# Start of a fused linear-attention and GEGLU kernel: weights' ends loaded once, loads reordered, one tile's statistics moved to ScalarE

## The chip, the cores and the metric

The kernel runs on one core of a Trainium2 chip. A core has a matrix engine (TensorE, PE in the profile), a vector engine (VectorE, DVE), an activation engine (ScalarE, ACT), a general engine (GpSimd, POOL) and a queue engine that issues most transfers (SyncE, SP). The metric is the device time of one execution in microseconds (us). The median of three runs before the change is 510.97 us (509.53 to 511.96).

## The reference

The input is `x`, 2048 tokens of 576 features in bf16. A layer norm without weights gives `xn`, which feeds two branches; their results and `x` are added.

```python
xn = (x - mean(x)) / sqrt(var(x) + 1e-5)
# branch A: linear attention, 32 heads of 18
q, k, v = split(xn @ wqkv)                      # wqkv 576 x 1728
phi = lambda t: where(t > 0, t + 1, exp(t)) + 1e-6
kv  = einsum("bhsd,bhse->bhde", phi(k), v)
z   = sum over tokens of phi(k)
o   = (phi(q) @ kv) / (phi(q) . z + 1e-6)
a   = o @ wo
# branch B: gated feed-forward, width 4608
b   = (gelu(xn @ w_gate) * (xn @ w_up)) @ w_down
out = x + a + b
```

Everything is in bf16 with float32 sums.

## The kernel before

The 2048 tokens are 16 tiles of 128. A tile's `x` is loaded, its mean and variance are taken (`ln_half`, two passes of 288 columns on VectorE, and `ln_aggr`), the reciprocal deviation is two short ScalarE instructions (`ln_rstd`, a logarithm and an exponential), and `ln_norm` writes the normalized tile to `xn`. GpSimd copies 64 columns of `x` next to the tile (`x_twin`), since the 576 features are held as five blocks of 128 with the last 64 doubled. The first four tiles are transposed on TensorE (`transposes`, ten small matmuls) and copied out of PSUM by ScalarE and VectorE, one half each (`tp_copy`); the other twelve are transposed by a DMA (`dma_transposes`).

A product of a transposed tile with weights is a unit of two accumulators. A contraction block of 128 rows is split in two halves of 64, which sit in different row halves of the array, so that two matmuls of 64 rows run side by side. A unit's first part (`rows`) has ten matmuls: five blocks for accumulator 0 in the low rows, and five for accumulator 1 in the high rows. The second part (`p2`) has the eight that remain, with the row halves exchanged; only the first four blocks are left then. So the last 64 rows of the weights (rows 512 to 575, called the ends here) are read by accumulator 0 in the low rows alone, and by accumulator 1 in the high rows alone. `_Token` is such a unit for K or Q of one tile (288 columns), `_Raw` one for gate and up of 128 feed-forward columns over 512 tokens.

The first stage of the program runs all K tiles, the first four Q tiles and 14 gate/up units on TensorE in the order that the list `line` gives: t0, K0, t1, K1, Q0, t2, Q1, t3, K2, K3, g0, g1, g2, g3, K4, g4, and so on to K15, Q2, Q3 (t is a transpose, g a gate/up unit; a unit's second part stands behind the next unit's first part). Between t0 and K0 stand ten matmuls that compute nothing (`row_spin`), and ahead of t0 stand 43 more (`spin(NWARM)`). A unit's accumulators stay in a pair of PSUM banks until a copy (`raw`, for K0, Q0, K1, Q1, K3), the feature map (`exp` on ScalarE, `clamp` and `phi` on VectorE, for the others) or a copy of gate and up (`out`) has read them; four pairs of banks go round. The sums of K over the tiles (z) are 15 additions on VectorE.

All steps of this stage but TensorE's own order are put in order by a planner (`in_order`): each step has an engine, a duration, a rank, the steps that it follows, and sometimes an earliest time (`X_AT`, `W_AT`, `DMA_FREE`, `LATER`), and each engine's instructions are emitted by the planned start. The numbers in it only set the order; on the chip each instruction waits for semaphores. The loads up to tile 9 and those of the first gate/up block (`load_gu(0, ...)`: the ends `wr` of gate and up, the main parts `wg` and `wu`) stand ahead of the plan in written order, nearly all on SyncE's queue. A load in this queue waits until the load eight places before it has landed; the count includes the one load of ScalarE's queue.

After that stage come the products with V through a Gram matrix (`gram`), and then four passes over 512 tokens each with the remaining gate/up units and the down projection. The change does not touch those.

Of the kernel before, what the change touches and what calls it, by code (L numbers as in the profile page):

```python
# [14 lines left out]
P = 128  # L15
# [22 lines left out]
NWARM = 43  # L38
# [8 lines left out]
LATER = 40.0  # L47

# [38 lines left out]
def kernel(  # L87
# [64 lines left out]
    xn = apool.tile([P, NS, XW], BF16, name="xn")  # L152
    g_sb = apool.tile([P, KT, D], BF16, name="g_sb")
# [6 lines left out]
    def load_w_main(which):  # L160
        c = slice(which * D, (which + 1) * D)
        nc.sync.dma_start(wqkv_sb[:, 0:4, c], A_wqkv[0:4 * P, c].rearrange("(kt p) c -> p kt c", p=P))
# [32 lines left out]
    load_w_main(1)  # L195
    load_w_last(1, LO)
    load_w_last(1, HI)
    load_x(2, 1)
    load_w_main(0)
    load_x(3, 1)  # L200
    load_w_last(0, LO)
    load_w_last(0, HI)
    load_x(4, 2)
    load_x(6, 2)
    load_gu(0, 0)
    load_gu(0, 1)
    load_x(8, 2)

    eps_ln = const.tile([P, 1], F32, name="eps_ln")
# [94 lines left out]

    def ln_aggr(n):
        nc.vector.bn_aggr(out=mv[:, n, :], in_=ln_raw[n][:])

    def ln_rstd(n, cnt):
        r = rstd[:, n:n + cnt]
        nc.scalar.activation(out=r, in_=mv[:, n:n + cnt, 1], func=ACT.Ln, bias=eps_ln[:], scale=1.0)  # L310
# [7 lines left out]
    def ln_norm(n):  # L318
# [4 lines left out]
        else:  # L323
            nc.vector.tensor_scalar(
                out=xn[:, n, :], in0=x_sb[:, n, :], scalar1=mv[:, n, 0:1], scalar2=rstd[:, n:n + 1],
                op0=ALU.subtract, op1=ALU.mult,
# [22 lines left out]
    X_AT = [3.35, 4.40, 7.10, 9.20]  # L349
    W_AT = {"K": 6.00, "Q": 8.80}  # L350
    DMA_FREE = 12.7
# [5 lines left out]
    for n, at in ((4, 10.2), (6, 11.2), (8, 14.5)):  # L357
        step(("x", n), "none", 0.0, 0, [], lambda: None, ready=at)
# [3 lines left out]
    for n in range(NS):  # L362
# [3 lines left out]
        x_at = X_AT[n] if n < 4 else 11.5 if n < 8 else 2.1 * both  # L366
        if n < 4:
            step(("twin", n), "POOL", 0.2, first, [], lambda n=n: x_twin(n, 1), ready=x_at)
        elif n == both:
            step(("twin", n), "POOL", 0.25, first, after_x, lambda n=n: x_twin(n, 2), ready=2.6 * n)  # L370
        twin = ("twin", n if n < 4 else both)
        for h in range(2):
            step(("stats", n, h), "DVE", 0.42, first, after_x, lambda n=n, h=h: ln_half(n, h), ready=5.1 if (n, h) == (1, 1) else x_at)
        step(("aggr", n), "DVE", 0.16, first, [("stats", n, 0), ("stats", n, 1)], lambda n=n: ln_aggr(n), tail=0.05)
# [20 lines left out]
    class _Token:  # L395

        def __init__(self, kind, n, ring=banks):
# [4 lines left out]
                lambda i, rows, kt: wqkv_sb[rows, kt, self.c + i * HALF:self.c + (i + 1) * HALF], nc.gpsimd, first=range(KT),  # L402
            )
            self.acc = ps_all[:, self.banks[0]:self.banks[0] + 2, :HALF]

# [65 lines left out]
    def p2_step(u):  # L471
        pe(("p2", u.name), u.t2, [("turn", u.name)], u.unit_p2)
        if u.name[0] in "KQ":
            later = u.name in RAW_T
            if later:
                step(("raw", u.name), "ACT", 0.66, u.at, [("p2", u.name)], u.body.raw, ready=11.4 if u.name == "K1" else 0.0)
# [10 lines left out]
    for name in line:  # L487
# [20 lines left out]
        else:  # L508
# [8 lines left out]
            at = 0.0 if blk else 9.1  # L517
# [414 lines left out]
```

## Time and profile before

| | |
|---|---|
| median of three runs | 510.97 us (509.53 to 511.96) |
| profiled execution, its own time | 509.63 us |
| its span | 507.8 us |
| TensorE busy | 502.7 us (99%) |
| VectorE busy | 228.7 us (45%) |
| ScalarE busy | 151.9 us (30%) |
| GpSimd busy | 8.2 us (2%) |
| bytes moved by DMA | 61.58 MB, mean 121 GB/s |

A line of the timeline has the start in us from the span's start, the duration, the engine, the line of the kernel, the operation, what is written and read, how many instructions were merged into the line (x10), and in brackets how long the engine sat idle before it and what ended that. SPq is SyncE's queue. Matmuls are pipelined: a line's duration holds the latency of its last matmul, so two starts tell more of the rate than a duration does. The end of a matmul is modelled; a gap between starts can be larger than the idle time that is shown.

### The profile page before, as it was taken

What the parts mean: (1) busy time and instruction counts of PE and PEld (TensorE: products, weight loads), DVE (VectorE), ACT (ScalarE), POOL (GpSimd) and SP (SyncE); (2) the same over time, 40 slices, a digit from 0 to 9 for tenths busy, and PEclk for the clock granted to TensorE, in tenths of its full rate; (3) what the DMA queues carried; (4) which work ended last, traced back from release to release, by engine and by line L of the source; (5) the groups of instructions that cost most, each with busy time, mean ns of one, the idle gap of its engine ahead of it and who ended that gap; (6) DMA issues with size and microseconds to landing.
All of it is one profiled execution on the core that took longest, in us unless ns stands there. A gap on an engine that the chain in (4) does not pass through costs nothing.

```text
span 507.8 us, 11198 instructions
## 1 busy us (share of the span) xinstructions
PE 502.7 (99%) x4772; PEld 305.6 (60%) x4772; DVE 228.7 (45%) x477; ACT 151.9 (30%) x265; POOL 8.2 (2%) x32
## 2 busy tenths in 40 slices
PE   8999999999999999999999999999999999999997
PEld 7566875446777444445777444445777444445774
DVE  5778966774101665543101665543101665543101
ACT  4888634335000532233000432233000432232000
POOL 2110000000000000000000000000000000000000
PEclk9999999999999999999999999999999999999999
DMA  9999906996200555654000455654000555640000
GB/s 263 239 220 241 266 1 180 248 269 121 71 13 25 145 150 156 176 163 108 12 13 25 142 151 152 179 162 109 14 12 26 144 151 156 175 112 14 13 13 23
DMA packets 113611, 61.58 MB, mean 121 GB/s; under 512 B 23250, under 2 KB 113562, under 8 KB 113562
## 3 DMA queue, kind: packets, MB, share of 16 engines
q1 hardware_dynamic: 113418, 60.72, 46.9%
q8 instruction: 37, 0.61, 0.5%
q10 hardware_dynamic: 144, 0.15, 0.1%
q14 instruction: 12, 0.10, 0.1%
HBM read 53.75 MB, written 2.36 MB: 110 GB/s over the span
## 4 chain that ended last, share of the span: by engine, by line
PE 94%; DVE 3%; DMA 2%; SPq 1%; issue 0%; ACT 0%; DVEq 0%
PE ps_all L252 58%; PE ps_all L847 28%; PE ps_all L558 3%; PE ps_all L852 3%; DVE hT L422 1%; DMA wu<-in_B_w_up_dram 1%; DMA wqkv_sb<-in_A_wqkv_dram 1%; DVE z_sum L529 1%; DVE phi_e L416 0%; PE ps_all L835 0%; PE ps_all L566 0%; DVE pq L422 0%; SPq L158 0%; PE ps_all L585 0%; PE ps_all L787 0%
## 5 line engine op out<-in xcount | busy, mean ns | idle before, releaser
L252 PE MATMUL ps_all<-xnT,wu 64*128 64x512 bf16 x1152 | 272.7, 376 | 0.3 <-DMA wu<-in_B_w_up_dram 0.3
L252 PE MATMUL ps_all<-xnT,wg 64*128 64x512 bf16 x1152 | 272.6, 376 | 0.0
L252 PEld LDWEIGHTS <-wu 64*128 64x128 bf16 x1152 | 107.9, 94 | 68.4 <-DMA wu<-in_B_w_up_dram 0.8
L252 PEld LDWEIGHTS <-wg 64*128 64x128 bf16 x1152 | 108.2, 94 | 65.2
L740 DVE TENSOR_TENSOR hT<-ps_all,gl 128x512 bf16<-128x512 f32 x130 | 89.9, 691 | 104.1 <-ACT gl L739 104.0
L847 PEld LDWEIGHTS <-hT 128*128 128x128 bf16 x1152 | 110.8, 98 | 30.9 <-issue 1.2
L739 ACT ACTIVATE gl<-ps_all 128x512 f32<-128x512 f32 x130 | 77.6, 597 | 164.1 <-PE ps_all L252 163.7
L861 DVE TENSOR_TENSOR res<-ps_all,x_sb 128x288 bf16<-128x288 f32 (+2 forms) x32 | 13.8, 455 | 146.3 <-PE ps_all L852 88.1
L847 PE MATMUL ps_all<-wd_a,hT 128*128 128x288 bf16 (+2 forms) x512 | 68.3, 286 | 0.0
L252 PE MATMUL ps_all<-xnT,wr 64*128 64x512 bf16 x288 | 57.3, 376 | 0.0
L847 PE MATMUL ps_all<-hT 128*128 128x288 bf16 (+2 forms) x384 | 52.4, 286 | 0.0
L761 ACT ACTIVATE gl<-ps_all 128x288 f32<-128x288 f32 x24 | 9.2, 410 | 121.4 <-PE ps_all L252 118.5
L847 PE MATMUL ps_all<-wd_m,hT 128*128 128x288 bf16 (+2 forms) x256 | 36.8, 286 | 0.0
L252 PEld LDWEIGHTS <-xnT 64*128 64x128 bf16 x576 | 32.6, 94 | 6.7 <-ACT xnT L344 0.9
L252 PE MATMUL ps_all<-wqkv_sb,xnT 64*128 64x288 bf16 x360 | 27.8, 283 | 0.7 <-ACT xnT L344 0.3
L252 PEld LDWEIGHTS <-wr 64*128 64x128 bf16 x288 | 15.2, 94 | 16.4
L852 PE MATMUL ps_all<-m_sb,pqT 128*128 128x288 bf16 (+2 forms) x128 | 20.9, 286 | 0.0
L558 PE MATMUL ps_all<-hT,xn 128*128 128x288 bf16 x128 | 16.0, 286 | 0.0
L437 ACT CAST hT<-ps_all 128x1024 bf16<-128x1024 f32 x14 | 14.1, 1010 | 4.0 <-PE ps_all L252 3.8
L558 PEld LDWEIGHTS <-xn 128*128 128x128 bf16 x128 | 12.4, 98 | 3.5 <-issue 0.5
L852 PEld LDWEIGHTS <-pqT 128*128 128x128 bf16 x128 | 12.4, 98 | 3.3
L303 DVE BATCH_NORM_STATS2 stats<-x_sb 128x6 f32<-128x288 bf16 x32 | 12.9, 435 | 2.9 <-DMA x_sb<-in_A_x_dram 2.9
(79 smaller groups left out, 228.4 us busy)
## 6 DMA issues: line engine op xcount, KB each, us to landing
wg<-in_B_w_gate_dram SPq DMA_DIRECT2D x72, 256.0 KB, 3.0
wu<-in_B_w_up_dram SPq DMA_DIRECT2D x72, 256.0 KB, 3.7
wr<-in_B_w_gate_dram SPq DMA_DIRECT2D x36, 64.0 KB, 3.2
wr<-in_B_w_up_dram SPq DMA_DIRECT2D x36, 64.0 KB, 2.9
wd_a<-in_B_w_down_dram SPq DMA_DIRECT2D x4, 576.0 KB, 8.2
out_dram<-res SPq DMA_DIRECT2D x15, 144.0 KB, 1.8
wqkv_sb<-in_A_wqkv_dram SPq DMA_DIRECT2D x3, 576.0 KB, 5.6
x_sb<-in_A_x_dram SPq DMA_DIRECT2D x6, 288.0 KB, 4.3
```

The source lines that it names most:

```text
L252: return nc.tensor.matmul(self.outs[i], lhsT=self.lhs(i, rows, kt), rhs=self.rhs(i, rows, kt), start=start, stop=stop, skip_group_check=True,)
L303: nc.vector.bn_stats(out=ln_raw[n][:, h, :], in_=x_sb[:, n, h * HALF:(h + 1) * HALF])
L422: nc.vector.scalar_tensor_tensor(out=dst[:, self.n, :].rearrange("p (h c) -> p h c", h=2), in0=self.acc, scalar=0.0, in1=self.e[:].rearran ...
L437: nc.scalar.copy(out=hT[:, self.f:self.f + NF + 1:NF, :], in_=ps_all[:, self.two[0]:self.two[0] + 2, :],)
L529: nc.vector.tensor_tensor(out=(z_bf if i == NS - 1 else z_sum)[:], in0=pk[:, z_order[0], :] if i == 1 else z_sum[:], in1=pk[:, z_order[i], :],
L558: nc.tensor.matmul(ps_all[:, two[hf], :HALF], lhsT=xn[:, n, kt * P:(kt + 1) * P], rhs=pk[:, n, hf * HALF:(hf + 1) * HALF], start=(n == 0), ...
L739: nc.scalar.activation(out=gl[:], in_=ps_all[:, b[0], :], func=ACT.Gelu_apprx_tanh)
L740: nc.vector.tensor_tensor(out=hT[:, GUB * k + i, :], in0=ps_all[:, b[1], :], in1=gl[:], op=ALU.mult)
L761: nc.scalar.activation(out=e[:, :HALF], in_=acc, func=ACT.Exp)
L847: nc.tensor.matmul(self.acc(hf), lhsT=hT[:, f, j * P:(j + 1) * P], rhs=wd(f)[:, self.parts[hf]], start=(f == 0 and not paired), stop=False ...
L852: nc.tensor.matmul(self.acc(hf), lhsT=pqT[:, c, self.ts], rhs=m_sb[:, c, self.parts[hf]], start=False, stop=(paired and c == 3), skip_grou ...
L861: nc.vector.tensor_tensor(out=self.res[:, hs], in0=self.acc(hf), in1=x_sb[:, self.n, hs], op=ALU.add)
```

## The change

- The ends of K's and Q's weights go to a tile of their own, `w_ends`. Each row half gets only the 288 columns that are read there. Before, both halves got all 576 columns.
- K's main rows come in two loads of two blocks each, with K's ends between them. The contraction order of a token's first part becomes 0, 1, 4, 2, 3 (before 0 to 4), and block 4 is read from `w_ends`.
- Q's ends stand ahead of tile 3 (before behind it), and the first gate/up block stands ahead of tiles 4 to 7 (before behind them).
- Tile 1's statistics are taken by two ScalarE passes: `act_sum` copies the tile with a running sum, GpSimd scales it to minus the mean (`act_mean`), and `act_square` squares the tile with that bias and again sums. `ln_rstd` and `ln_norm` of this tile follow with a scale of 1/576 and an addition in place of the subtraction.
- 40 empty matmuls at the start (before 43).
- Times in the planner are changed, and the eighth addition of z also follows the feature map of K13.

```diff
-NWARM = 43
+NWARM = 40
+ACT_STATS = 1
...
+    w_ends = apool.tile([P, 2, HALF], BF16, name="w_ends")
...
-    def load_w_main(which):
+    def load_w_main(which, k0=0, k1=4):
...
+    def load_w_ends(which):
+        for i, rows in enumerate((LO, HI)):
+            c = which * D + i * HALF
+            nc.sync.dma_start(w_ends[rows, which, :], A_wqkv[512:576, c:c + HALF])
...
-    load_w_main(1)
-    load_w_last(1, LO)
-    load_w_last(1, HI)
+    load_w_main(1, 0, 2)
+    load_w_ends(1)
+    load_w_main(1, 2, 4)
     load_x(2, 1)
     load_w_main(0)
+    load_w_ends(0)
     load_x(3, 1)
-    load_w_last(0, LO)
-    load_w_last(0, HI)
+    load_gu(0, 0)
+    load_gu(0, 1)
     load_x(4, 2)
     load_x(6, 2)
-    load_gu(0, 0)
-    load_gu(0, 1)
     load_x(8, 2)
...
+    def act_sum(n):
+        nc.scalar.activation(out=xn[:, n, 0:D], in_=x_sb[:, n, 0:D], func=ACT.Copy, accum_out=act_acc[:])
+    def act_mean(n):
+        nc.gpsimd.tensor_scalar(out=mv[:, n, 0:1], in0=act_acc[:], scalar1=-1.0 / D, scalar2=None, op0=ALU.mult)
+    def act_square(n):
+        nc.scalar.activation(
+            out=xn[:, n, 0:D], in_=x_sb[:, n, 0:D], func=ACT.Square, bias=mv[:, n, 0:1], accum_out=mv[:, n, 1:2],
+        )
...
-    X_AT = [3.35, 4.40, 7.10, 9.20]
-    W_AT = {"K": 6.00, "Q": 8.80}
-    DMA_FREE = 12.7
+    X_AT = [3.35, 3.75, 6.70, 9.10]
+    W_AT = {"K": 6.00, "Q": 8.70}
+    DMA_FREE = 13.6
...
+        if n == ACT_STATS:
+            step(("sum", n), "ACT", 0.62, first - 3.0, [], lambda n=n: act_sum(n), ready=x_at)
+            step(("mean", n), "POOL", 0.27, first - 3.0, [("sum", n)], lambda n=n: act_mean(n))
+            step(("aggr", n), "ACT", 0.62, first, [("mean", n)], lambda n=n: act_square(n))
...
-                lambda i, rows, kt: wqkv_sb[rows, kt, self.c + i * HALF:self.c + (i + 1) * HALF], nc.gpsimd, first=range(KT),
+                self.weights, nc.gpsimd, first=(0, 1, 4, 2, 3),
...
+        of += [("phi", "K13")] * (i == 8)
```

In the built program the plan changes the order on three engines. ScalarE has: the first pass of tile 1, `rstd` of tile 0, the second pass, `rstd` of tile 1, and only then the copy of the transposed tile 0; before, that copy stood right behind `rstd` of tile 0. VectorE has the normalization of tile 2 ahead of tile 3's statistics, before it stood behind them; and behind K12's feature map one addition of z stands ahead of K13's, before three did. Ahead of K13's feature map stand 7 additions in all, before 9. TensorE's order is the same.

## The prediction

> **What bounds the kernel.** I read the page's busy times first, then the chain, then the timeline of the first 15 us engine by engine, then the stretch around 55 us.
>
> ```profile
> span 507.8 us, 11198 instructions
> PE 502.7 (99%) x4772; PEld 305.6 (60%) x4772; DVE 228.7 (45%) x477; ACT 151.9 (30%) x265; POOL 8.2 (2%) x32
> ```
>
> TensorE is the bound, and its arithmetic does not change. All the change can touch are TensorE's pauses in the first stage, so I list them. Starts tell more than durations here: 36 matmuls of 288 columns, 18 pairs, begin at 11.84 and the next group at 14.04, so a pair takes 0.122 us.
>
> ```profile
> 5.89 0.44 PE L236 MATMUL ps_all<-warm 64*128 64x128 bf16 x10
> 6.60 0.79 PE L252 MATMUL ps_all<-wqkv_sb,xnT 64*128 64x288 bf16 x10 [0.26 <-ACT xnT L344]
> 7.54 0.32 PE L339 MATMUL ps_all<-ident,xn 64*128 64x64 bf16 x10 [0.16 <-DVE xn L324]
> 7.70 0.65 PE L252 MATMUL ps_all<-wqkv_sb,xnT 64*128 64x288 bf16 x8
> ...
> 10.31 0.32 PE L339 MATMUL ps_all<-ident,xn 64*128 64x64 bf16 x10
> 10.47 1.27 PE L252 MATMUL ps_all<-wqkv_sb,xnT 64*128 64x288 bf16 x18
> 11.57 0.31 PE L339 MATMUL ps_all<-ident,xn 64*128 64x64 bf16 x10
> 11.84 2.38 PE L252 MATMUL ps_all<-wqkv_sb,xnT 64*128 64x288 bf16 x36
> 14.04 0.40 PE L252 MATMUL ps_all<-xnT,wr 64*128 64x512 bf16 x2
> 14.26 0.38 PE L252 MATMUL ps_all<-xnT,wg 64*128 64x512 bf16 x1
> 14.91 0.39 PE L252 MATMUL ps_all<-xnT,wu 64*128 64x512 bf16 x1 [0.27 <-DMA wu<-in_B_w_up_dram]
> ```
>
> K0 starts at 6.60 behind ScalarE's copy of the transposed tile. Its five pairs are issued by 7.21; the transpose of tile 1 follows at 7.54 (0.33 open). K0's second part is issued by 8.19 and K1 starts at 8.58 (0.39 open). From there to 14.26 only 0.11 is open, at 11.84. Gate/up pairs later follow each other at 0.215, so the pair of 14.26 should be followed at 14.48; it is followed at 14.91, since `wu` had not landed: 0.43 lost. Then TensorE has no pause until 55 us:
>
> ```profile
> 54.73 0.56 PE L252 MATMUL ps_all<-wqkv_sb,xnT 64*128 64x288 bf16 x5
> 55.45 0.30 PE L252 MATMUL ps_all<-wqkv_sb,xnT 64*128 64x288 bf16 x2 [0.16 <-DVE hT L422]
> ```
>
> The five end their issue at 55.13, so 0.32 is lost to a feature map (L422), K13's, which holds the banks that Q2 needs. VectorE shows why it is late:
>
> ```profile
> 51.31 0.76 DVE L422 SCALAR_TENSOR_TENSOR hT<-ps_all,phi_e 128x576 bf16<-128x576 f32 x1
> 51.98 2.33 DVE L529 TENSOR_TENSOR z_sum<-z_sum,hT 128x576 f32<-128x576 f32 x3
> 54.23 0.30 DVE L416 TENSOR_SCALAR phi_e<-phi_e 128x576 bf16<-128x576 bf16 x1
> 54.64 0.76 DVE L422 SCALAR_TENSOR_TENSOR hT<-ps_all,phi_e 128x576 bf16<-128x576 f32 x1
> ```
>
> Three additions of z stand in front of it. Another 0.1 is open at 58.25, where the Gram products wait behind K14's map. So what can be won is 0.43 + 0.32 + 0.10, and something of the 0.83 before 12 us: 1.7 us at the very most, a third of a per cent.
>
> **Loads.** K's and Q's ends shrink by 72 KB each. Main rows of K in two: K0 was not waiting for weights but for ScalarE, and the second half lands near 6.2 (864 KB of loads were in by 5.91, now 936 KB stand up to there, at some 300 GB/s). Price: nothing; the cover is ScalarE's copy. The first gate/up block passes tiles 4 to 7 (576 KB), and 144 KB are gone ahead of it: 720 KB at 300 GB/s is 2.4 us, so `wu` lands near 12.5 in place of 14.86, and the 0.43 goes with about 1.8 us to spare. What is late next is tile 4: GpSimd's copy saw it at 10.40; 640 KB more and 144 less stand before it, 1.65 us, so about 12.1. Its normalization moves from 13.42 to about 14.2, and its DMA transpose, issued from 13.89 to 15.45 before, ends issuing near 16.3. Issue to landing of these took 4.0 to 5.8, so it lands by 20.3 to 22.1; K4 started at 21.89. The queue ahead of it is shorter by 144 KB (0.5 us), so I take no stall; the bound is 0.4.
>
> SyncE's own wait also moves. The second of Q's ends waited 0.8 us for K's main load; now it waits for half of that, which has landed. Tile 4 now waits for Q's main load, near 8.4, with tiles 6 and 8 and the second gate/up block behind it. The transfers issued earlier keep the engines fed until 12.5, so this costs nothing.
>
> **Tile 1's statistics.** VectorE loses 0.41, 0.46 and 0.21, which lay in its waits. ScalarE gains two passes on the path:
>
> ```profile
> 4.46 0.29 ACT L310 ACTIVATE rstd<-mv,eps_ln 128x1 f32<-128x1 f32 x1 [2.37 <-DVE mv L306]
> 4.78 0.20 ACT L311 ACTIVATE rstd<-rstd 128x1 f32<-128x1 f32 x1
> 6.09 0.43 ACT L344 COPY xnT<-ps_all 128x320 bf16<-128x320 bf16 x1 [1.10 <-PE ps_all L339]
> 6.41 0.30 ACT L310 ACTIVATE rstd<-mv,eps_ln 128x1 f32<-128x1 f32 x1
> ```
>
> An exponential over 128x576 from SBUF takes 0.67; a bias pointer costs 0.09 (0.29 against 0.20). So the passes are 0.67 and 0.76 without the running sum. For that no row exists: between 0 (it writes besides, so it cannot save) and 0.20 (one more short instruction); I take 0.10, the middle, as neither row is nearer. Tile 1 lands at 3.76 (issued 1.06, 2.7 to landing). First pass 3.80 to 4.57; `rstd` of tile 0 to 5.12 (4.98 before); GpSimd's mean, 0.26 like its other one-column step, is hidden under it (behind it in GpSimd's queue stand the copies of tiles 2 and 3, which land after 6.4 and so wait for nothing); second pass 5.15 to 6.02; `rstd` 1 to 6.57; only now the copy of tile 0, to 7.03: K0 starts at 7.11 in place of 6.60. But tile 1 is normalized meanwhile (to 7.12, before 7.49), so its transpose follows K0 directly at 7.72 (7.54), and its two copies end at 8.50: K1 starts at 8.60, as before (8.58). The loss of 0.51 is absorbed by the pauses of 0.33 and 0.39.
>
> Then tile 3: its statistics wait for tile 2's normalization (9.10 to 9.55), so 9.58 in place of 9.09; aggregate 10.60 (10.37), `rstd` 11.17 (10.93), normalized 11.70 (11.48), transpose 11.80 (11.57). K1's raw copy stands behind that `rstd` on ScalarE and frees K2's banks at 12.1 (11.79). K2 at 12.15, and g0 at 14.35, where before it was effectively 14.04 + 0.43 = 14.47. Gain at the start: 0.12; 0.3 if the running sum is free, and 0.1 lost if it costs 0.20.
>
> The Trainium skill, "ScalarE: Activation LUTs", section "What ACT_TABLE_LOAD costs", gives 186 ns + 0.833 per column and 93 ns for each pointer: 0.67 and 0.76, by which the sum would be the same. Its section "Rules for kernel authors" sends plain arithmetic to VectorE rather than ScalarE, which speaks against this part.
>
> **The z additions.** Two fewer stand ahead of K13's map, 0.75 each, so it is ready 1.5 us earlier than 55.40 on VectorE, and its producer allows that: the K13 exponential can follow its second part, issued by 53.2. Both pauses, 0.32 and 0.10, go. Two additions now stand before K14's map, as before.
>
> **Empty matmuls.** They are 0.107 apart, so three fewer end 0.32 earlier, at about 5.5; nothing waits for them. The transposes of tile 0 come at 5.88. The price is nothing unless the clock minds the pause.
>
> **Sum.** 0.12 + 0.32 + 0.10 = 0.54, say 0.55. The profiled execution's 509.63 would become 509.1. It lies 1.34 below the median of the runs shown, which becomes 510.4.
>
> **Rivals.**
>
> *The clock comes late, slower.* The empty matmuls of 128 columns start 0.107 apart up to 5.51; the spin's pairs of 128 columns at 5.89 take 0.056. So the array doubles its rate about 4.6 us after its start at 1.06. If the pause near 5.6 made that time begin anew, the rate would rise at about 10.3: K0, K1, Q0 and K1's second part, 23 pairs, would take 0.244 instead of 0.122, so 2.8 us more, less 0.6 of pauses filled: 2.2, net 1.65 slower, 512.6. It decides against the change once the rate rises after about 8.5. Against it: the pause is 0.4 against 4.5 us of activity.
>
> The Trainium skill, "TensorE: Matmul & The Clock Gate", Part 1, says the clock is released after a busy window of about 3.4 us that runs free of the kernel's start, with shifts of half a us from run to run; by it a 0.4 us pause within a window might or might not count. [...]
>
> *ScalarE's two passes cost the whole start.* With 0.20 for each running sum and tile 2's chain late by as much again, g0 starts at 14.9, losing 0.4 where I win 0.12: only z remains, 0.0 net, 511.0.
>
> *Tiles 4 to 7 late.* Their transposes land after K4 wants them: up to 0.4 for one, 0.9 if x4 meets the queue later: 510.8 to 511.3.
>
> *More is won.* The running sum is free, x2 and Q land 0.2 earlier and the chain up to K3 moves as a whole: 0.85 + 0.35 = 1.2, 509.8.
>
> **How the numbers follow.** My forecast 0.60 (its own range 509.9 to 510.9 without the spread of runs), ScalarE's cost 0.12, more won 0.11, clock 0.09, late tiles 0.08. What a measurement can tell is about 0.5%, 2.55 us; runs before spread 1.2 each way, so a median of a few runs may shift by 1. No case reaches 2.55 by itself. The low end is the larger gain with such a shift, 508.7; the high end the late clock, 512.6. Faster 0.06 (the larger gain with a lucky median), slower 0.08 (the late clock with an unlucky one), same 0.86.
>
> **What would show it.** Right: no wait of the first gate/up unit for `wu`, g0 near 14.3, K0 near 7.1 behind ScalarE, no pause at 55. Wrong: a wait of K4 for its transposed tile, matmuls of K0 at 0.24 a pair, or ScalarE passes above 1 us.

## The result and the profile after

The changed kernel takes 510.95 us (median of 22 executions, 510.14 to 511.67), the kernel before beside it on the same chip 509.72 (509.33 to 511.96): the ratio is 1.0022 with a 95% interval of 1.0015 to 1.0028, so 1.1 us slower where 0.55 faster was forecast. The time lies inside the forecast range, but the change went the other way than forecast. The profiled execution took 510.90, against 509.63 of the one before: +1.27. A few single executions of the kernels below took 527 to 1889 us; they are left out of all medians and ratios.

The head of its page, busy time by engine:

```profile
span 509.0 us, 11195 instructions
PE 502.1 (99%) x4769; PEld 304.5 (60%) x4769; DVE 227.6 (45%) x474; ACT 153.7 (30%) x269; POOL 8.7 (2%) x33
```

TensorE is busy a little less than before (502.1, before 502.7) in a span that is 1.2 longer: the difference is waiting. TensorE's timeline of the first 16 us (the columns as in front):

```profile
5.59 0.32 PE L359 MATMUL ps_all<-ident,xn 64*128 64x64 bf16 x10 [0.74 <-DVE xn L344]
5.74 0.44 PE L243 MATMUL ps_all<-warm 64*128 64x128 bf16 x10
6.68 0.42 PE L259 MATMUL ps_all<-wqkv_sb,xnT 64*128 64x288 bf16 x4 [0.49 <-ACT xnT L364]
...
8.82 0.42 PE L259 MATMUL ps_all<-wqkv_sb,xnT 64*128 64x288 bf16 x4 [0.58 <-ACT rstd L328]
...
9.81 0.42 PE L259 MATMUL ps_all<-wqkv_sb,xnT 64*128 64x288 bf16 x4 [0.19 <-DMA wqkv_sb<-in_A_wqkv_dram]
...
12.79 0.32 PE L359 MATMUL ps_all<-ident,xn 64*128 64x64 bf16 x10 [0.23 <-DVE xn L344]
...
15.30 0.40 PE L259 MATMUL ps_all<-xnT,wr 64*128 64x512 bf16 x2
15.51 0.38 PE L259 MATMUL ps_all<-xnT,wg 64*128 64x512 bf16 x1
15.53 0.38 PE L259 MATMUL ps_all<-xnT,wu 64*128 64x512 bf16 x1
```

K0 starts at 6.68, not at the 7.11 that was forecast. K1, at 8.82, starts 0.74 after what precedes it has been issued; Q0 at 9.81 waits 0.36 for Q's weights (0.11 more inside the group that follows); the transpose of tile 3 at 12.79 has 0.39 open. The first gate/up unit begins at 15.30 instead of 14.04, and its pair of `wg` and `wu` now follows at once: the wait of 0.43 is gone. Together the start is 1.26 - 0.43 = 0.83 later. A second wait is new:

```profile
24.39 0.38 PE L259 MATMUL ps_all<-xnT,wg 64*128 64x512 bf16 x1
25.41 0.39 PE L259 MATMUL ps_all<-xnT,wu 64*128 64x512 bf16 x1 [0.65 <-DMA wu<-in_B_w_up_dram]
```

The pair should have followed at 24.60; `wu` of the second block came at 25.37, and 0.81 is lost. The pause of 0.32 near 55 is gone (between 53 and 58.2 matmuls follow each other without one); the 0.10 in front of the Gram products is still there, now at 59.55. Sum: 0.83 + 0.81 - 0.32 = 1.32, against 1.27 measured. So there are two losses to explain, one ahead of 15 us and one at 25.

Where the first comes from is seen in the transfers. Busy time by stretch, with the share of the 16 DMA engines and GB/s at the end of each line; first the kernel before, then the changed one:

```profile
4.00:5.00 1.00, 1.00 (x13) 1.00 (x11) 0.71 (x3) 0.50 (x2) 0.00 (x1) 1.00 1.08 386
5.00:6.00 1.00, 1.00 (x22) 0.82 (x22) 0.88 (x3) 0.00 (x0) 0.00 (x0) 1.00 1.08 305
6.00:7.00 1.00, 0.74 (x22) 0.56 (x16) 0.45 (x2) 0.82 (x3) 0.23 (x1) 1.00 1.08 353
```

```profile
4.00:5.00 1.00, 0.84 (x15) 0.67 (x12) 0.39 (x2) 0.97 (x5) 0.24 (x2) 1.00 0.86 125
5.00:6.00 1.00, 0.41 (x20) 0.42 (x20) 0.47 (x2) 0.97 (x3) 0.00 (x0) 1.00 1.16 320
6.00:7.00 1.00, 0.51 (x14) 0.28 (x10) 0.74 (x2) 0.59 (x3) 0.00 (x0) 1.00 0.67 153
```

From 4 to 5 us the engines move 125 instead of 386 GB/s, though they count as busy for 0.86 of the time, and from 6 to 7 they move 153 instead of 353. These are the stretches right behind K's two halves, which land at 4.57 and 6.17. The packets tell what the busy time is: of those of 1152 bytes (one row), the median takes 51 ns in both kernels; from 3.5 to 7.5 us one packet of the kernel before takes over 250 ns, and 31 of the changed one do (30 rows of 1152 bytes and one of 576), 269 to 1044 ns each, 16.4 us in all or 1.0 us for each of the 16 engines. So less is loaded and it lands later. GpSimd's copies show when a tile is there (x2, x3, x4), before and after:

```profile
6.76 0.24 POOL L330 COPY x_sb<-x_sb 128x64 bf16<-128x64 bf16 x1 [2.76 <-DMA x_sb<-in_A_x_dram]
9.12 0.24 POOL L330 COPY x_sb<-x_sb 128x64 bf16<-128x64 bf16 x1 [2.12 <-DMA x_sb<-in_A_x_dram]
10.40 0.30 POOL L330 COPY x_sb<-x_sb 128x128 bf16<-128x128 bf16 x1 [1.04 <-DMA x_sb<-in_A_x_dram]
```

```profile
7.46 0.24 POOL L350 COPY x_sb<-x_sb 128x64 bf16<-128x64 bf16 x1 [2.61 <-DMA x_sb<-in_A_x_dram]
10.59 0.24 POOL L350 COPY x_sb<-x_sb 128x64 bf16<-128x64 bf16 x1 [2.90 <-DMA x_sb<-in_A_x_dram]
14.69 0.30 POOL L350 COPY x_sb<-x_sb 128x128 bf16<-128x128 bf16 x1 [3.87 <-DMA x_sb<-in_A_x_dram]
```

Q's main rows land on the first of the 16 engines at 8.20 and on the last at 9.77 (before 7.76 and 8.47). The Trainium skill, "DMA: Bandwidth & Descriptors", section "Queues, rings and completion order", says that one copy is split over up to 16 rings, one on each of the DMA engines, and that each engine takes the descriptors of its ring in order; the sixteen landings of this load, 1.57 apart, agree. A load counts as landed with its last engine.

K1's wait is x2's delay at second hand. VectorE's timeline of the changed kernel:

```profile
7.43 0.82 DVE L310 BATCH_NORM_STATS2 stats<-x_sb 128x6 f32<-128x288 bf16 x2 [0.58 <-DMA x_sb<-in_A_x_dram]
8.28 0.21 DVE L324 BATCH_NORM_AGGREGATE mv<-stats 128x2 f32<-128x12 f32 x1
8.41 0.27 DVE L364 COPY xnT<-ps_all 128x320 bf16<-128x320 bf16 x1
```

The copy of the transposed tile 1, which K1 needs, stands behind tile 2's statistics in VectorE's order, and these waited for x2. The plan put them so because it took x2 to be there at 6.70. (K1's own line names an `rstd` of ScalarE as what released it, but K1 starts 0.14 after the end of this copy at 8.68; in the kernel before the copy ended at 8.44 and K1 started at 8.58, the same 0.14.)

The second loss begins at SyncE's queue (issue of transfers):

```profile
9.78 1.40 SPq L160 DMA_DIRECT2D x_sb<-in_A_x_dram  x3
...
13.13 0.51 SPq L160 DMA_DIRECT2D x_sb<-in_A_x_dram  x1
16.86 1.68 SPq L367 DMA_TRANSPOSE xnT<-xn  x1
18.59 0.57 SPq L187 DMA_DIRECT2D wr<-in_B_w_gate_dram  x1
```

x4 is issued at 9.78 (6.45 before), as soon as Q's main rows, eight loads ahead, have landed. It lands at 14.64, and that is one engine's doing: on fifteen engines it is there by 13.78. It is normalized from 16.39 on, and its DMA transpose, which the queue reached at 13.64, goes out at 16.86 (13.89 before). Behind it stand the second block's weights: `wr` at 18.59 (15.51), `wu` at 21.78 (18.69), landing at 25.37 (23.06).

ScalarE did what it was meant to:

```profile
3.76 0.68 ACT L313 ACTIVATE xn<-x_sb 128x576 bf16<-128x576 bf16 x1 [1.69 <-DMA x_sb<-in_A_x_dram]
4.35 0.18 ACT L313 ACTIVATION_READ_ACCUMULATOR xn<-x_sb 128x1 f32 x1
4.46 0.29 ACT L328 ACTIVATE rstd<-mv,eps_ln 128x1 f32<-128x1 f32 x1
4.78 0.20 ACT L331 ACTIVATE rstd<-rstd 128x1 f32<-128x1 f32 x1
4.89 0.76 ACT L319 ACTIVATE xn<-x_sb,mv 128x576 bf16<-128x576 bf16 x1
5.56 0.19 ACT L319 ACTIVATION_READ_ACCUMULATOR xn<-x_sb,mv 128x1 f32 x1
5.78 0.29 ACT L328 ACTIVATE rstd<-mv,eps_ln 128x1 f32<-128x1 f32 x1
6.11 0.20 ACT L331 ACTIVATE rstd<-rstd 128x1 f32<-128x1 f32 x1
6.21 0.41 ACT L364 COPY xnT<-ps_all 128x320 bf16<-128x320 bf16 x1
```

A running sum adds an instruction of 0.18 to 0.19, but it starts under the end of its pass: the `rstd` of tile 0 still begins at 4.46, exactly as before. In the same way the copy that K0 needs starts at 6.21, while the `rstd` in front of it runs to 6.31. Instructions on ScalarE overlap, and the forecast added whole durations: that is why K0 came at 6.68 and not at 7.11.

### The profile page after: what moved, and what is told of

Read it like the earlier page. It is cut to its first block, busy times and chain, and to the rows that moved or that the text cites. A ratio compares the mean times of both kernels' runs of the same rounds, so it can differ in the third digit from the quotient of the medians.

```text
span 509.0 us, 11195 instructions
## 1 busy us (share of the span) xinstructions
PE 502.1 (99%) x4769; PEld 304.5 (60%) x4769; DVE 227.6 (45%) x474; ACT 153.7 (30%) x269; POOL 8.7 (2%) x33
## 4 chain that ended last, share of the span: by engine, by line
PE 94%; DMA 3%; SPq 1%; DVE 1%; issue 0%; ACT 0%; DVEq 0%
PE ps_all L259 59%; PE ps_all L878 28%; PE ps_all L589 3%; PE ps_all L883 3%; DMA wqkv_sb<-in_A_wqkv_dram 1%; DMA x_sb<-in_A_x_dram 1%; DMA wu<-in_B_w_up_dram 1%; PE ps_all L866 0%; PE ps_all L597 0%; SPq L367 0%; PE ps_all L616 0%; DVE stats L310 0%; SPq L169 0%; SPq L164 0%; PE ps_all L818 0%
```

## The experiments

The theory that these readings give: K's main rows in two loads make all transfers behind them later, which is the first loss; tile 4 behind the first gate/up block, and its transpose at the head of SyncE's queue, is the second. Rivals: the narrow ends (loads of 64 rows of 576 bytes) are what slows the transfers; ScalarE's passes cost the start; SyncE takes 0.4 to 0.6 us for each load whatever its size, so one load more makes all behind it late by that (the issue); the plan or the missing empty matmuls do it.

All kernels here have plain copies in place of the 28 DMA transposes (12 of `xn`, 16 of the attention result), as the first expectation says; they are compared with the base, copy_before, which is the kernel before with that edit alone. All ratios are to the kernel before, run beside them. Each kernel has one profiled execution, and its time is given where it is among the longest of its kernel; copy_ends_scalar_t4 has no usable trace.

**The base and the whole change.**

```diff
-        nc.sync.dma_start_transpose(xnT[:, :, n * P:(n + 1) * P], xn[:, n, :])
+        nc.sync.dma_start(xnT[:, :, n * P:(n + 1) * P], xn[:, n, :].rearrange("p (k t) -> p k t", t=P))
...
-        nc.sync.dma_start_transpose(pqT[:, :, n * P:(n + 1) * P], den_pn[n][:])
+        nc.sync.dma_start(pqT[:, :, n * P:(n + 1) * P], den_pn[n][:].rearrange("p (k t) -> p k t", t=P))
```

> The kernel before with its 28 transposing DMAs (12 of xn, 16 of the attention result) replaced by plain DMAs that copy the tile without transposing it; the transposition of tiles 4 to 15 and of the attention result is left out, so the output is not the reference's. It is the base for the runs beside it, which all leave the same out. Up to 13.9 us nothing differs from the kernel before: tile 2 landed at 6.71, Q's main rows at 8.47, tile 3 at 9.07, the up weights of the first block at 14.86. The time should be within 1 us of the kernel before, as TensorE has no pause between 15 and 55 us that the transposes could cause.

Measured: 510.01 us, ratio 1.0004 (0.9995 to 1.0013), with the pauses of the kernel before: 0.29 at 7.32, 0.39 at 8.36, 0.31 at 14.68, 0.32 at 55.22. It stands for the kernel before.

> The changed kernel with the same replacement. If the loss is made at the start (theories A and B below), g0 starts near 15.3 as in the changed kernel's profile and the time is 0.5 to 1.3 us above the base beside it; the wait of 0.81 near 25 us may shrink, since a plain copy holds the queue for less time. If the whole loss came from the transposing DMAs behind the reordered loads, the time is at or below the base (0 to 0.5 less).

Measured: 510.11, ratio 1.0007 (0.9998 to 1.0016). The first loss is there (Q lands from 8.03 to 9.79, base 7.70 to 8.24; first gate/up unit at 15.16, base 13.94 and a wait of 0.31), and the pause at 55 is gone. The second is not, in the profiled execution: x4 came at 13.66, and a plain copy holds the queue for 0.71 where the DMA transpose held it for 1.68. So with copies the whole change costs 0.0003 in the ratio, less than the intervals can tell; what follows is about its pieces, whose effects are larger.

**K in one load; the halves next to each other.** Two kernels from copy_after:

```diff
-    load_w_main(1, 0, 2)
-    load_w_ends(1)
-    load_w_main(1, 2, 4)
+    load_w_main(1)
+    load_w_ends(1)
```

> The changed kernel, same replacement, with K's main rows in one load again (576 KB) and K's ends (72 KB) behind it. In the changed kernel tile 2 landed at 7.41 us (6.71 before), Q's main rows at 9.77 (8.47), tile 3 at 10.54 (9.07), tile 4 at 14.64 (10.35), and the packets show two thin stretches, 4.25 to 5.0 and 6.0 to 7.25. Theory A (the split empties the transfer engines: the first 288 KB are through at 4.6, and the next big load was only issued at 2.96, behind two small ones of 0.57 and 0.59 of queue time): with one load both thin stretches go, tile 2 lands near 6.6, Q near 8.4, tile 3 near 9.1, tile 4 near 12.3; g0 starts near 14.2 without a wait and the time is 0.4 to 1.0 us below the base. Theory B (ScalarE's two passes or the narrower ends slow the transfers): thin stretches and time as in the changed kernel. Theory C (gate/up ahead of tiles 4 to 7 does the harm by itself): tile 3 near 9.1, yet a wait for weights near 25 us and a time at the base or above it.

Measured: 509.88, ratio 1.0006 (0.9996 to 1.0015). x2 lands at 6.29 (copy_after 6.85), Q's last engine at 8.92 (9.79); K1 follows without a pause and the first gate/up unit starts at 14.24, 0.92 earlier than in copy_after. The engines are still 1.5 us apart at Q. The gain doesn't reach the end, since the second loss now shows:

```profile
24.24 0.39 PE L258 MATMUL ps_all<-xnT,wu 64*128 64x512 bf16 x1 [0.53 <-DMA wu<-in_B_w_up_dram]
```

0.69 is lost there: x4 came at 13.54, its copy was issued at 15.75, with the queue free since 12.50. So the two losses are separate: in these executions K whole removes the first and not the second.

```diff
     load_w_main(1, 0, 2)
-    load_w_ends(1)
     load_w_main(1, 2, 4)
+    load_w_ends(1)
```

> The changed kernel, same replacement, with K's two halves one behind the other and the ends behind both. Theory A (the engines run dry because two small loads stand between the halves): as with one load, tile 2 near 6.7, tile 3 near 9.1, 0.3 to 1.0 us below the base. A variant of A (every further load costs a gap of its own, whatever stands between): the thin stretches stay in whole or in half, time at the base or up to 1.2 above. Theory B: as the changed kernel.

Measured: 510.00, ratio 1.0006 (0.9998 to 1.0015). Its profiled execution, at 510.76 the second longest of its eleven, has x2 at 8.01 and Q from 7.57 to 10.07. In this execution it does not help the loads behind the halves that these follow each other at once.

**The issue.** From copy_after, halves adjacent, and the ends of K and Q in two loads on ScalarE's queue, so that SyncE issues Q at 2.98 instead of 4.09:

```diff
-    def load_w_ends(which):
+    def load_w_ends(on):
+        both = A_wqkv[512:576, 0:2 * D].rearrange("p (w c) -> p w c", w=2)
         for i, rows in enumerate((LO, HI)):
-            c = which * D + i * HALF
-            nc.sync.dma_start(w_ends[rows, which, :], A_wqkv[512:576, c:c + HALF])
+            on.dma_start(w_ends[rows, :, :], both[:, :, i * HALF:(i + 1) * HALF])
...
     load_x(1, 1, nc.scalar)
+    load_w_ends(nc.scalar)
     load_w_main(1, 0, 2)
-    load_w_ends(1)
     load_w_main(1, 2, 4)
```

> The changed kernel with plain copies in place of the transposing DMAs (left out as in the base), and the ends of K and Q in two loads (both weights' columns of one row half in each) issued by ScalarE's queue behind tile 1; the other loads on SyncE's queue as changed. Theory D (issue): a load takes SyncE about 0.5 us whatever its size and its bytes flow about 2 us later; the four loads of 36 KB take 2.3 us of the queue and are moved in 0.5, so the engines catch up with the queue, and every load behind is late. Then tile 2 lands near 6.1 (6.85 in the changed kernel with copies, 6.51 in the base), Q near 8.0 (9.79, 8.24), tile 3 near 8.6 (10.40, 8.97), g0 starts near 13.9 to 14.2, and the time is 0.4 to 1.0 us below the base. Theory B (rows of 576 bytes slow the engines themselves): thin stretches right behind the ends remain, tile 3 no earlier than 9.5, time at the base or above. In both ScalarE's first pass must not start later than 3.8.

Measured: 509.15, ratio 0.9992 (0.9983 to 1.0001), 0.8 us below copy_after. But its profiled execution is the longest of its eleven (510.12) and shows no better landings: x2 8.04, Q 7.73 to 10.10 although issued 1.1 us earlier. So in this execution an early issue alone did not make Q land early behind two halves of K. Why the median is low can't be read from this trace; it shows that in this order of issue the change, with K in two halves, lies no higher than the base.

```diff
-        ("x", 10), ("xnT", 4), ("gu", 2, 0), ("xnT", 5), ("gu", 2, 1), ("x", 12), ...
+        ("x", 10), ("gu", 2, 0), ("gu", 2, 1), ("xnT", 4), ("xnT", 5), ("x", 12), ...
```

> As the run beside it, and the third gate/up block's loads moved ahead of tile 4's and tile 5's copies in SyncE's queue. In the changed kernel SyncE stood still from 13.6 to 16.9 us in front of tile 4's transposing DMA, and the up weights behind it came 0.8 us late. Theory (the queue's head waits for tile 4's normalization and holds back the weights): where the run beside it still has a wait for up weights between 20 and 26 us, this one has none, and is faster by that wait, 0 to 0.7 us; K4 must not begin to wait for its tile. If the weights were late for want of transfer speed, the wait stays.

Measured: 509.14, ratio 0.9988 (0.9978 to 0.9997). With the second block ahead of tile 4's copy the time is that of copy_ends_scalar within its spread; without a trace it says nothing on where.

**ScalarE's passes.** From copy_after, `ACT_STATS = 1` becomes `-1`.

> The changed kernel with copies, and tile 1's statistics on VectorE again. Theory D: the landings of the changed kernel with copies (tile 2 near 6.9 to 7.4, Q near 9.8, tile 3 near 10.4) stay, and so does the time, within 0.3 us of the changed kernel with copies. Theory B' (ScalarE's passes, from 3.76 to 4.5 and 4.9 to 5.75, disturb the transfers at 4.25 to 7.25): landings as in the base, time 0.3 to 1.0 below.

Measured: 511.17, ratio 1.0029 (1.0017 to 1.0040), 1.1 us above copy_after: taking the passes away makes it worse. The thin transfers stay (29 packets over 250 ns from 3.5 to 7.5 us, copy_after 19), and 0.79 at 25.54 waits for the second block, which is most of the difference. The passes are not the cause.

**The narrow ends.** On the base, narrow ends alone (`w_ends` and `load_w_ends` as in the change, in the places of the wide loads):

> The base (kernel before with plain copies) with the ends alone changed: K's and Q's ends as four loads of 64 rows of 576 bytes, at the places where the wide ones stood. So far every kernel with these narrow loads, wherever they stood and whichever queue issued them, had transfer engines that fall behind each other: Q's main rows land over 1.5 to 2.5 us from the first engine to the last (0.4 to 0.7 in the base), and tile 3 by 9.5 to 10.7 (8.8 to 9.1). Theory N (the narrow rows upset the engines): Q lands over more than 1.2 us, tile 3 after 9.4, and the time is 0.3 to 1.0 us above the base. Theory S (the split of K's rows does it): spread below 0.8, tile 3 by 8.9 (72 KB less stand ahead of it), time within 0.3 of the base.

Measured: 509.32, ratio 0.9993 (0.9984 to 1.0001), Q from 7.60 to 8.29, x2 6.59. They are harmless; a gain is not shown, as the interval overlaps the base's. The other way round, copy_after with the wide ends in the same places:

> The changed kernel with plain copies and with wide ends (both row halves get all 576 columns, as in the kernel before) at the places of the changed kernel. Theory N: Q lands within 0.8 us, tile 2 near 6.6, tile 3 near 9.1, the time 0.5 to 1.2 us below the changed kernel with copies. Theory S (split and order): tile 2 at 6.9 or later, spread above 1.2, time as the changed kernel with copies or above.

Measured: 511.35, ratio 1.0029 (1.0017 to 1.0041), Q from 8.04 to 10.32, x4 15.82. Wide ends don't cure the split; beside it they cost 0.22% more than the narrow ones. And copy_after with each weight's ends as one load of 128 rows:

```diff
-        for i, rows in enumerate((LO, HI)):
-            c = which * D + i * HALF
-            nc.sync.dma_start(w_ends[rows, which, :], A_wqkv[512:576, c:c + HALF])
+        nc.sync.dma_start(
+            w_ends[:, which, :], A_wqkv[512:576, which * D:(which + 1) * D].rearrange("p (i c) -> i p c", i=2),
+        )
```

> The changed kernel with plain copies and the ends of each weight as one load of 128 rows of 576 bytes (both row halves at once), two loads in place of four. If the length of a row is what upsets the engines, all stays as in the changed kernel with copies (spread of Q's landing 1.5 us or more). If it is the number of short loads (64 rows, four for each engine, with a signal at the end of each) or their queue time, the spread falls below 1.0, tile 2 lands by 6.6 and the time is 0.5 to 1.0 us lower.

Measured: 511.20, ratio 1.0027 (1.0017 to 1.0038), x2 7.80, Q from 7.34 to 9.68, x3 11.69. There are two loads fewer in the queue, but this kernel changes more than their number: each of the two new loads is signalled by two engines only, where the others are by sixteen. K's ends land at 6.06 and 6.64, Q's at 10.69 and 11.39, after Q's main rows, and TensorE waits for them:

```profile
11.43 0.30 PE L259 MATMUL ps_all<-w_ends,xnT 64*128 64x288 bf16 x2 [1.18 <-DMA w_ends<-in_A_wqkv_dram]
```

So it does not tell what fewer loads are worth. The Trainium skill, "DMA: Bandwidth & Descriptors", section "Rules for kernel authors", advises one 128-partition transfer in place of two for the two halves of the partitions; no run here shows that for a load that all sixteen engines share.

**The split alone.** On the base, K's main rows in two loads with the wide ends between them, nothing else:

```diff
-    load_w_main(1)
+    load_w_main(1, 0, 2)
     load_w_last(1, LO)
     load_w_last(1, HI)
+    load_w_main(1, 2, 4)
```

> The base with one edit: K's main rows in two loads with K's wide ends between them. Theory N: landings as in the base to 0.3 us, spread below 0.8, time within 0.3 us of the base. Theory S: a thin stretch from 4.6 us on, tile 2 near 7.0 to 7.4, Q's landing spread above 1.2, time 0.5 to 1.3 us above the base.

Measured: 511.32, ratio 1.0027 (1.0016 to 1.0039): 0.23% or 1.2 us above the base from one load cut in two. Its stretch from 4 to 5 us, and TensorE:

```profile
4.00:5.00 1.00, 1.00 (x13) 1.00 (x11) 0.64 (x3) 0.50 (x2) 0.01 (x1) 1.00 0.94 166
```

```profile
8.67 0.79 PE L253 MATMUL ps_all<-wqkv_sb,xnT 64*128 64x288 bf16 x10 [0.23 <-DVE mv L307]
10.70 0.67 PE L253 MATMUL ps_all<-wqkv_sb,xnT 64*128 64x288 bf16 x8 [1.24 <-DMA wqkv_sb<-in_A_wqkv_dram]
```

The thin stretch (166 against the base's 385) is the changed kernel's, with Q on its first engine at 7.98 and on its last at 10.66, and TensorE pays 1.41 at 10.70 for it; its first gate/up unit starts at 16.11, 2.17 later than the base's (the profiled execution, 511.66, is the second longest of seven). So cutting this load is enough for late landings and a later start, with wide ends and on the base; copy_k_one_load showed the other way round that the late start goes when K is whole. The split with narrow ends alone on the base was not run, and copy_after and copy_ends_scalar have it among other edits with no loss against the base: what a cut costs in time depends on what else is changed.

**What in the split.** Two kernels on the base. K as three blocks and one:

```diff
-    load_w_main(1)
+    load_w_main(1, 0, 3)
     load_w_last(1, LO)
     load_w_last(1, HI)
+    load_w_main(1, 3, 4)
```

> Base, with K's main rows in two loads of unequal size: rows 0 to 383 (432 KB), the two wide ends, and rows 384 to 511 (144 KB) behind them. In copy_split_on_before halves of 288 KB gave 1.0027, a thin stretch of 162 KB from 4 to 5 us and 2.7 us between Q's first and last engine. Theory of the lead (a load must be issued well before the transfers ahead of it end, or engines stand empty): the first part lasts 1.5 us instead of 1.0, so the thin stretch comes about half as deep (230 KB or more in its thinnest us), Q spreads by 1.3 or less and the time is 0.2 to 0.9 us above the base (ratio 1.0005 to 1.0015). Theory of any boundary in K: as copy_split_on_before, Q's spread above 2 us, ratio 1.0022 to 1.0032.

Measured: 510.37, ratio 1.0014 (1.0004 to 1.0023). The median lies between base and even split, and its interval overlaps the base's. The landings are no better than in the even split: Q spreads from 8.07 to 10.68, and the thin stretch has only moved a microsecond on (234 GB/s from 5 to 6, 122 from 6 to 7). But they are those of an execution of 511.85, the second longest of twelve, so they don't explain the median.

K whole, and two tiny loads ahead of Q:

```diff
+    for i in range(2):
+        nc.sync.dma_start(small[LO, i, :], A_wqkv[512:576, 32 * i:32 * i + 32])
     load_w_main(0)
```

> Base, with K whole, and two additional small loads (64 rows of 64 bytes each, into a tile that nothing reads) between tile 2 and Q's main rows on SyncE's queue: 8 KB in all, but Q, tile 3 and all behind them are issued about 1.1 us later. Theory of the lead: Q's issue moves from about 3.6 to about 4.8, a thin stretch appears where K and tile 2 end (below 200 KB in one us from 6 to 8), Q's last engine lands at 9.0 or later, tile 3 at 9.6 or later, time 0.4 to 1.3 us above the base (ratio 1.001 to 1.0025). Theory that the cut of K itself is what costs: landings within 0.3 us of the base, Q's spread below 0.9, ratio 0.999 to 1.0008.

Measured: 510.32, ratio 1.0009 (1.0000 to 1.0017). 8 KB move Q's issue from 3.6 to 4.74 and its last engine from 8.24 to 9.00; from 6 to 7 us 151 GB/s flow, and 15 packets over 250 ns appear without any cut in K (base 2). So a thin stretch comes with a late issue, too. But the engines stay together (Q 8.45 to 9.00), and the median is 0.3 us above the base's, with intervals that overlap. So a late issue may explain a part; that after a cut in K the engines come apart by 1.6 to 2.7 us is not explained by it.

Packets of weights and tiles over 250 ns from 3.5 to 7.5 us, counted from the traces' packet records:

```
K whole:  before 1, copy_before 2, copy_before_narrow 2, copy_narrow_z 4, copy_whole_mid 4,
          copy_narrow_z_mid 8, copy_k_one_load 10, copy_two_small 15
K split:  copy_ends_scalar 13, copy_after_wide 17, copy_k_adjacent 18, copy_after 19,
          copy_after_ends_128 19, copy_split_31 22, copy_split_on_before 26, copy_stats_vector 29, after 31
```

**The edge in the chain of z.** On the base:

```diff
-    step(("z", i), "DVE", 0.76, 80.0, of + ([("z", i - 1)] if i > 1 else []), lambda i=i: z_add(i))
+    step(("z", i), "DVE", 0.76, 80.0, of + ([("z", i - 1)] if i > 1 else []) + [("phi", "K13")] * (i == 8), lambda i=i: z_add(i))
```

> The base (kernel before with plain copies) with one edit: the eighth addition of z also follows the feature map of K13, so that one addition instead of three stands ahead of that map on VectorE. By the prediction's step the pauses of 0.32 us near 55 and 0.10 near 58 go and nothing else changes: 0.3 to 0.45 us below the base. Rival: the additions only move the pause to the Gram products (K14's map, 58 us): the sum stays within 0.1.

Measured: 509.47, ratio 0.9997 (0.9989 to 1.0006). TensorE's timeline near 55:

```profile
53.75 4.00 PE L252 MATMUL ps_all<-wqkv_sb,xnT 64*128 64x288 bf16 x61
57.80 0.90 PE L558 MATMUL ps_all<-hT,xn 128*128 128x288 bf16 x6
```

61 matmuls without a pause, so the 0.32 is gone, but the Gram products start 0.22 behind their issue instead of 0.10: the additions moved behind K13's map now stand in front of the next one. 0.2 is won, not 0.42.

**What is left when the harm is left out.** Narrow ends and the edge of z on the base; then the first gate/up block also ahead of tiles 6 and 7, but not of 4 and 5:

> Two parts of the change alone, K in one load: the narrow ends (copy_before_narrow: 0.9993) and the edge of K13's map in the chain of z (copy_before_z: 0.9997). If their gains add: 0.4 to 0.6 us below the base, ratio to the kernel before 0.9988 to 0.9994, no pause at 55, about 0.2 at 58. If not: as copy_before_narrow alone.

Measured: 509.23, ratio 0.9989 (0.9980 to 0.9997); no pause at 55, 0.22 at 57.87, the wait for `wu` 0.54 at 14.74.

```diff
     load_x(4, 2)
-    load_x(6, 2)
     load_gu(0, 0)
     load_gu(0, 1)
+    load_x(6, 2)
```

> As copy_narrow_z, with the first gate/up block ahead of tiles 6 and 7 only, tiles 4 and 5 where they were. 288 KB less stand before the block, so wu of block 1 lands near 13.5 in place of 14.45 and the wait of 0.10 to 0.31 near 14.5 goes; x4 stays near 10.5, so its transposed copies and block 2's weights are issued as in the base, and no wait opens at 22 to 26. Expected 0.1 to 0.4 us below copy_narrow_z, ratio 0.998 to 0.9988. Rival: tile 6 and its normalization come 1 us later and the queue's head waits there instead; then block 2 is late again and the gain is gone (ratio 0.999 to 1.0003).

Measured: 509.04, ratio 0.9989 (0.9981 to 0.9998). The wait at 14.74 is gone and none opens before 57, but beside copy_narrow_z the measurement can't tell them apart. Last, all of the change except the split of K and the place of tiles 4 and 5:

> All parts of the change but two: K's main rows stay one load, and the first gate/up block goes ahead of tiles 6 and 7 only, with tiles 4 and 5 (and their times in the plan) ahead of it. It is copy_narrow_z_mid with tile 1's statistics on ScalarE and 40 empty matmuls. If the two left out are all that did harm: x4 lands by 11.0, no wait of a gate/up unit before 30 us, K0 near 6.6, Q lands with a spread below 1.0, ratio 0.9975 to 0.9988, which is 0.1 to 0.6 us below copy_narrow_z_mid. If ScalarE's passes gain nothing once the loads come as in the base: ratio 0.9987 to 0.9992. If something else of the change does harm (the plan, the missing empty matmuls): above 0.9995.

Measured: 508.65 us, ratio 0.9979 (0.9970 to 0.9988). Transfers, VectorE and TensorE of it:

```profile
4.00:5.00 1.00, 1.00 (x13) 1.00 (x11) 0.43 (x2) 0.97 (x5) 0.27 (x2) 1.00 1.08 375
```

```profile
6.80 0.81 DVE L309 BATCH_NORM_STATS2 stats<-x_sb 128x6 f32<-128x288 bf16 x2
7.65 0.21 DVE L323 BATCH_NORM_AGGREGATE mv<-stats 128x2 f32<-128x12 f32 x1
7.78 0.27 DVE L363 COPY xnT<-ps_all 128x320 bf16<-128x320 bf16 x1
```

```profile
13.71 0.40 PE L258 MATMUL ps_all<-xnT,wr 64*128 64x512 bf16 x2
13.93 0.38 PE L258 MATMUL ps_all<-xnT,wg 64*128 64x512 bf16 x1
13.95 0.38 PE L258 MATMUL ps_all<-xnT,wu 64*128 64x512 bf16 x1
```

The stretch behind K is full, tile 2's statistics start at 6.80, where in the changed kernel they waited to 7.43, with the same order on VectorE, and the copy behind them is in time. The first gate/up unit starts at 13.71 with its weights there, and no wait opens at 25. It is 0.25% or 1.3 us below the base, and the whole interval lies below both kernels. Together with whole K, the rest of the plan, the 40 empty matmuls and ScalarE's passes do no harm; against copy_narrow_z_mid, which lacks the passes, it is 0.1% lower, with intervals that overlap. With the DMA transposes in place of the copies this version was not tried.

## Why the prediction was wrong

**K's main rows in two loads: "Price: nothing; the cover is ScalarE's copy." This is the step that failed.** The cover was looked for in K0's own wait, and K0 indeed did not wait: it started behind ScalarE's copy, and the second half landed at 6.17, as forecast ("near 6.2"). What was not asked is what the cut does to the loads behind it. x2 came 0.70 later, Q 1.30, x3 1.47, and the first gate/up unit 0.83, where 0.12 was to be won. copy_split_on_before shows the like with the split alone (1.2 us above the base). The rate of some 300 GB/s was taken as a property of the engines that any order of loads keeps; right behind the first half it was 125.

**"The transfers issued earlier keep the engines fed until 12.5, so this costs nothing", and tile 4 "near 12.1".** The wait was seen at the right place, x4 behind Q's main rows, but Q landed at 9.77 rather than near 8.4, x4 was issued then, and it landed at 14.64. **"So I take no stall; the bound is 0.4"** failed with it: the forecast looked at K4, which needs the transposed tile, and K4 did not wait. Here what waited was what stands behind the transpose in SyncE's queue, the second block's weights: 0.81 at 25.41. The rival "tiles 4 to 7 late" had the right cause and nearly the right price (0.4 to 0.9), and named the wrong victim. copy_k_one_load has this loss without the split (0.69); copy_whole_mid, with x4 in its old place, has neither.

**`wu` lands "near 12.5", the 0.43 goes.** Right: 12.65, and no wait.

**ScalarE's passes.** The durations were right (0.68 and 0.76 for 0.67 and 0.76). The running sum was put at 0.10; it is an instruction of 0.18 to 0.19 of which 0.02 shows behind the first pass and 0.13 behind the second, counted to the start of the next. K0 came at 6.68, better than the forecast 7.11, since the instructions overlap. K1 at 8.60 was wrong (8.82) by way of x2. So the rival "ScalarE's two passes cost the whole start" is refuted, also by copy_stats_vector (1.1 us worse without them).

**Additions of z.** The 0.32 went as forecast; the 0.10 in front of the Gram products did not. The forecast took it for a wait on K14's map. But that map ended 0.31 ahead of the Gram products in the kernel before (57.94 and 58.25) and 0.69 ahead in the changed one (58.86 and 59.55), and in both their first weight load stands 0.24 behind the one in front of it, with nothing shown that released it:

```profile
58.25 1.83 PEld L558 LDWEIGHTS <-xn 128*128 128x128 bf16 x16 [0.24 <-issue]
```

```profile
59.54 0.48 PEld L589 LDWEIGHTS <-xn 128*128 128x128 bf16 x5 [0.24 <-issue]
```

So moving additions could not win it. Only in copy_before_z does the map come last (it ends at 57.75, and the products start at 57.80), and there the pause grew to 0.22, behind a map with three additions ahead of it.

**Empty matmuls and the clock.** Right in that no rate was lost: K0's pairs are 0.12 to 0.13 apart (6.68, 6.93 for two pairs, 7.06). But the pause was longer than thought. The spacing of the empty matmuls fell from 0.107 to 0.056 us already at 4.01, 2.96 after the first of them; in the kernel before it was still 0.107 at the last of them, 4.45 after the first. So the empties ended earlier, and TensorE stood still for 0.74 ahead of 5.59 instead of 0.4. Here the faster spacing came ahead of the pause; in copy_whole_mid, where it was 0.107 to the last of the 40, K0's pairs are 0.12 apart all the same.

**The sum.** Forecast -0.12 - 0.32 - 0.10; measured +0.83 + 0.81 - 0.32 + 0. The first two came from the two failed steps; without them a gain was left, as copy_whole_mid shows with copies. That 510.95 lies near the forecast time of 510.4 is luck: the forecast was reckoned from 510.97, the median of three executions of the kernel before, which took 509.72 beside the change, and the difference between the two kernels has the wrong sign.

**What stays open.** Why a cut in K slows packets behind it and drives the engines 1.6 to 2.7 us apart. A late issue may do a part (copy_two_small). An earlier issue (copy_ends_scalar) and a longer first part (copy_split_31) did not bring the landings back in the executions that were profiled; but the median of copy_ends_scalar, 0.9992, lies no higher than the base's, and what makes up for the cut there is open. And K whole is not all that keeps the engines together: in copy_k_one_load they were 1.5 apart at Q, in copy_whole_mid, with the same loads up to tile 3, 0.85. Nor do the experiments have the DMA transposes: with copies in their place the whole change costs nothing that can be told (1.0007 against 1.0004), though in the profiled executions copy_after is 0.38 above the base (509.72 and 509.34), with the first loss in its trace. So that the two losses together make the 1.1 us was read from the trace of the changed kernel; neither was taken away there.

## What to carry to other kernels

A load that is cut so that its consumer may start early has to be judged by the loads behind it, too: look at the GB/s of the microsecond after the cut, and at the first and the last engine's landing of the next large load. When a transfer is moved back in a queue, follow not only its own consumer but whatever stands behind the instruction that needs it; a waiting transpose at a queue's head delayed weights that have nothing to do with it. And where an order was planned on a landing time, one late landing holds all that stands behind it in that engine's order, here a copy that had been ready for 0.8 us.

## What the runs showed of the hardware

- In the kernel before, the loads from 4 to 9 us run at 260 to 386 GB/s with packets of 51 ns a row; behind a cut, single packets of the same size take 250 to 1500 ns, and engines count as busy in them (share 0.86 at 125 GB/s).
- SyncE takes about 0.4 to 0.6 us to issue a load, whatever its size here: 0.41 for 576 KB of K, 0.60 for 4 KB in copy_two_small.
- A running sum on ScalarE is an instruction of its own, 0.18 to 0.19, which starts under the end of its pass (0.02 and 0.13 of it show).
- A packet of 16 KB of the instruction queue takes 0.91 to 1.54 us and starts at 9.98 to 13.07 us in all eighteen traces (both kernels and the sixteen with copies). Behind it one engine is late: in the kernel before it takes 1.18 from 10.81, and of the sixteen landings of the first block's `wu` fifteen come by 13.55 and the last at 14.86; in the changed kernel it takes 1.11 from 11.57, and of x4's landings fifteen come by 13.78 and the last at 14.64. That the one makes the other was not tested.
